# Attention and two expert layers on one core: single conversion steps, a norm by 32x32 transposes, operands split in the first phase

## The chip, the core and the metric

The kernel runs on one core of a Trainium2 chip. The core has five engines with a queue each: TensorE (PE in the rows, its weight loads PEld), VectorE (DVE), ScalarE (ACT), GpSimd (POOL) and SyncE (SP), whose queue issues the DMAs here. Each engine works through its queue in order; an instruction waits for semaphores that others raise. Matrix products write to PSUM, here to tiles of 512 float32 columns. The metric is the device time of one execution in microseconds; the median of three runs of the kernel before is 1184.3 us (1182.97 to 1186.25).

## The reference

```python
def _attn_ref(q, k, v, tau):            # q, k, v: 1 x 6016 x 256
    qn = q / (np.linalg.norm(q, axis=1, keepdims=True) + 1e-06)
    kn = k / (np.linalg.norm(k, axis=1, keepdims=True) + 1e-06)
    s = kn.transpose(0, 2, 1) @ qn / tau
    s = s - s.max(-1, keepdims=True)
    a = np.exp(s)
    a /= a.sum(-1, keepdims=True) + 1e-09
    return (v @ a).astype(np.float32)
# x = _attn_ref(...) as 6016 x 256, then
def _moe_ref(x, w_in, w_out):           # 256 -> 2048 -> 256
    h = np.maximum(x @ w_in, 0.0)
    return (h * h @ w_out).astype(np.float32)
def _moe2_ref(x, w_gate, w_val, w_out, rms_g):   # 256 -> 1536 -> 256
    rms = np.sqrt(np.mean(x * x, axis=-1, keepdims=True) + 1e-06)
    xn = x / rms * rms_g
    g = xn @ w_gate
    silu = g * (1.0 / (1.0 + np.exp(-g)))
    return (silu * (xn @ w_val) @ w_out).astype(np.float32)
```

`w_in`, `w_out`, `w_gate`, `w_val` and the second `w_out` (`w2` in the kernel) arrive as float64 and are converted on the chip.

## The kernel before

**Precision.** A float32 product is made of three products of rounded halves: `mm3` (L95 to L98) multiplies the high half of the weights by the high and by the low half of the data, then the low half of the weights by the high half of the data. A high half is a cast to `fp32r` (ACT), a low half the difference between the value and its cast (DVE): the helper `split`, L91 to L93.

**Start.** `q` and `k` are read in chunks and give the 256 x 256 scores; the softmax gives the matrix `a`. Since `v @ a @ w_in` is linear up to the relu, `a` is multiplied into `w_in` (`emit_m`, tiles `m_h`, `m_l`).

**Weights.** Each piece of a float64 weight goes through five stages (class `Call`): `load` (SP), `a` (POOL and ACT take the two words of each number), `b` in three DVE instructions `b0`, `b1`, `b2`, `h` (the high half, ACT) and `l` (the low half, DVE). Gate and value weights (class `Pieces`) are also combined on POOL into seven blocks (for a scheme of seven instead of eight products of 2 x 2 blocks), of which the first two chunks stay in SBUF and the others are stored to DRAM through the tile `gp` with two buffers. `tick` runs the stages of one weight together.

**First phase.** The 6016 tokens are 12 blocks: ten of 512 and two of 448. A block goes through 16 units (function `unit`, L630 ff.): `up` is one 128-row strip of the hidden layer (6 matmuls), then `read` takes it from PSUM with a relu (ACT, `r`), squares it (`s`, on ACT in odd units, on DVE in even ones) and casts the square (`sh`, ACT); `rest` makes the low half `sl` (DVE, L691); `down` multiplies both into two sums `y` (6 matmuls). `pending` holds `down` back by two units. Blocks 0 and 1 run interleaved, blocks 2 to 11 one after the other. A unit takes further work by `hooks` (ahead of `read`), `mid` (behind it) and, from L700 on, functions returned by the hooks, that run last: the transposes and splits of the next block of `v` (`prep`), `tick` in units 1 and 5, the norm of the block before, and the operands of the pair before.

**Norm and operands.** `norm_steps` copies `y` from PSUM, squares both halves (ACT), adds them (DVE), splits the sum and multiplies it by a matrix of 1/256 (L745, L746, two matmuls of 512 columns), so that each of 128 rows holds the mean; then come a square root (ACT), four reciprocals of a quarter each (L753) and two multiplications (L759). Two blocks make a pair: with four differences on POOL (`pair_steps`, L774) the seven operands of the seven products are complete and are stored to DRAM as one DMA (L780).

**Second phase.** Six pairs, each in 12 groups (function `group`). A group makes seven products of three matmuls (L841) into four banks, combines them on DVE (`u`, `h22`, `h21`, `h12`), applies silu on ACT, and splits the results into `sh` and `sl`; four `down` of three matmuls fall into the group's slots, delayed by some slots. Operands of the next pair are fetched in group 9 as one tile (L811) and split in group 11, each behind its last product, by a cast on ACT and a difference on POOL (`split_op`, L817, L818). The sums of a pair are read from PSUM by DVE transposes (`finish`, L924) in the first two groups of the next pair, two in each.

The order of the work is the order of the Python code: each engine's queue holds its instructions as they are emitted. A tile is given again when all uses of the tile before in the same buffer are done.

## Time and profile before

| | |
|---|---|
| median of three runs | 1184.3 us |
| profiled execution, and its span | 1183.07 us, 1181.3 us |
| busy: TensorE, VectorE, ScalarE, GpSimd | 96%, 75%, 56%, 13% |
| granted TensorE clock, mean | 0.992 of 2.4 GHz |
| DMA | 79.66 MB, mean 67 GB/s |

The span runs from the first to the last instruction of one profiled execution. Lines such as L691 are lines of the kernel before. In the names of tiles, `mm` and `acc` are PSUM banks. By the timeline the start takes about 62 us, the first phase reaches to about 613 us, the second to the end. A row of waits names the instruction that waited, the instruction for which it waited, the total, the number of times and the longest. The clock of a window is the mean of what was granted in it: 1.00 is 2.4 GHz, and 0.50 the lower level, 1.2 GHz.

### The profile page before, as it was taken

To read this page: it belongs to the slowest core of one execution; us is meant where nothing else is said; L and a number is where in the kernel's file an instruction comes from. 1 tells how busy PE (TensorE), PEld (TensorE's weight loads), DVE (VectorE), ACT (ScalarE), POOL (GpSimd) and SP (SyncE) were. 2 spreads that over 40 slices of the span, in tenths; PEclk is the share of its full clock that TensorE was granted. 3 is DMA by queue.
4 is the path that set the end of the run, shared out by engine and by line. 5 is a ranking of instruction groups with operands and counts; after the bars stand their busy time and mean duration, and the time that the engine had idled before them with its cause. 6 is when DMAs were issued, how large, how long until landed. Compare 5 with 4: busy or idle time off the path is not lost.

```text
span 1181.3 us, 14492 instructions
## 1 busy us (share of the span) xinstructions
PE 1136.7 (96%) x5220; PEld 946.0 (80%) x5220; DVE 891.7 (75%) x1319; ACT 661.6 (56%) x1144; POOL 150.6 (13%) x142
## 2 busy tenths in 40 slices
PE   8999979999999999999999999999999999999996
PEld 7978858787887878889987787887887787787895
DVE  7987778766866866665647879779778778878875
ACT  7787778577677576566675344334334334334332
POOL 0121120401201210200211112003003003003000
PEclk9999989999999999999999999999999999999999
DMA  9853332313223120100323303001100200300101
GB/s 291 219 141 90 90 83 79 115 46 117 73 62 98 57 86 16 63 16 1 125 96 154 117 1 90 9 1 38 61 1 19 81 1 4 88 1 1 36 1 32
DMA packets 85289, 79.66 MB, mean 67 GB/s; under 512 B 56032, under 2 KB 70880, under 8 KB 83552
## 3 DMA queue, kind: packets, MB, share of 16 engines
q1 hardware_dynamic: 85216, 78.72, 22.0%
q8 instruction: 41, 0.67, 0.2%
q14 instruction: 32, 0.26, 0.1%
HBM read 54.43 MB, written 24.28 MB: 67 GB/s over the span
## 4 chain that ended last, share of the span: by engine, by line
PE 75%; DVE 10%; issue 5%; ACT 5%; DMA 3%; SPq 2%; POOL 1%; DVEq 0%; ACTq 0%; POOLq 0%
PE mm L841 24%; PE acc L97 10%; PE acc L96 10%; PE acc L98 10%; PE mm L96 6%; PE mm L97 6%; PE mm L98 6%; DVE hp L905 1%; DVE sl L896 1%; DVE hp L882 1%; SPq L325 1%; DVE hp L871 1%; DVE hp L881 1%; DVE pu L869 1%; ACT sh L892 1%
## 5 line engine op out<-in xcount | busy, mean ns | idle before, releaser
L841 PE MATMUL mm<-o,gv 128*128 128x512 f32 (+1 forms) x1512 | 388.7, 388 | 9.6 <-DVE hp L871 5.1
L841 PEld LDWEIGHTS mm<-o,gv 128*128 128x128 f32 x1512 | 283.4, 188 | 70.7 <-DVE hp L871 8.9
L691 DVE TENSOR_TENSOR sl<-o,sh 128x512 fp32r<-128x512 f32 (+1 forms) x192 | 141.3, 736 | 114.9 <-ACT sh L684 102.7
L679 ACT ACTIVATE o<-mm 128x512 f32<-128x512 f32 (+1 forms) x192 | 112.6, 587 | 126.6 <-PE mm L98 125.1
L892 ACT CAST sh<-hp 128x512 fp32r<-128x512 f32 (+1 forms) x144 | 88.2, 612 | 169.7 <-DVE hp L882 102.2
L97 PE MATMUL acc<-sl,wo_h 128*128 128x512 f32 (+1 forms) x384 | 151.4, 394 | 6.2 <-DVE sl L691 6.2
L96 PE MATMUL mm<-o,m_h 128*128 128x512 f32 (+1 forms) x384 | 149.3, 389 | 4.7 <-ACT o L92 4.7
L96 PE MATMUL acc<-sh,wo_h 128*128 128x512 f32 (+1 forms) x384 | 150.1, 391 | 1.5 <-ACT sh L687 1.5
L98 PE MATMUL acc<-sh,wo_l 128*128 128x512 f32 (+1 forms) x384 | 149.2, 388 | 0.2 <-DVE wo_l L160 0.2
L98 PE MATMUL mm<-o,m_l 128*128 128x512 f32 (+1 forms) x384 | 148.8, 388 | 0.3 <-DVE m_l L621 0.3
L97 PE MATMUL mm<-o,m_h 128*128 128x512 f32 (+1 forms) x384 | 149.0, 388 | 0.0
L879 ACT ACTIVATE sg<-mm 128x512 f32<-128x512 f32 (+1 forms) x72 | 42.3, 588 | 136.5 <-PE mm L841 136.5
L896 DVE TENSOR_TENSOR sl<-hp,sh 128x512 fp32r<-128x512 f32 (+1 forms) x144 | 108.5, 754 | 12.0 <-ACT sh L892 7.4
L96 PE MATMUL acc<-sh,w_h 128*128 128x512 f32 (+1 forms) x288 | 112.0, 389 | 4.2 <-DVE ot L924 4.2
L818 POOL TENSOR_TENSOR o<-xs,o 128x512 fp32r<-128x512 f32 (+1 forms) x42 | 60.3, 1461 | 409.5 <-ACT o L817 409.2
L97 PE MATMUL acc<-sl,w_h 128*128 128x512 f32 (+1 forms) x288 | 112.0, 389 | 0.3 <-DVE sl L896 0.2
L98 PE MATMUL acc<-sh,w_l 128*128 128x512 f32 (+1 forms) x288 | 111.0, 385 | 0.0
L97 PEld LDWEIGHTS acc<-sl,wo_h 128*128 128x128 f32 x384 | 72.7, 189 | 21.7 <-DVE sl L691 8.9
L881 DVE TENSOR_TENSOR hp<-mm,pu 128x512 f32<-128x512 f32 (+1 forms) x72 | 48.8, 678 | 54.1 <-PE mm L841 54.1
L96 PEld LDWEIGHTS mm<-o,m_h 128*128 128x128 f32 x384 | 72.6, 189 | 19.6 <-ACT o L92 5.2
L96 PEld LDWEIGHTS acc<-sh,wo_h 128*128 128x128 f32 x384 | 72.7, 189 | 17.4 <-ACT sh L687 3.1
L686 DVE TENSOR_TENSOR o<-o 128x512 f32<-128x512 f32 (+1 forms) x88 | 64.5, 732 | 27.9 <-ACT o L679 26.6
(132 smaller groups left out, 1728.8 us busy)
## 6 DMA issues: line engine op xcount, KB each, us to landing
xd<-xst SPq DMA_DIRECT2D x5, 1792.0 KB, 6.7
raw<-in_moe_w_out_dram SPq DMA_DIRECT2D x14, 512.0 KB, 3.8
gv<-gvd SPq DMA_DIRECT2D x4, 1792.0 KB, 9.8
xs<-xd SPq DMA_DIRECT2D x4, 1792.0 KB, 7.2
gvd<-gp SPq DMA_DIRECT2D x12, 512.0 KB, 3.3
out_dram<-ot SPq DMA_DIRECT2D x40, 128.0 KB, 2.5
qraw<-in_q_dram SPq DMA_DIRECT2D x13, 384.0 KB, 5.3
qraw<-in_k_dram SPq DMA_DIRECT2D x13, 384.0 KB, 6.0
```

Source lines behind the costliest of these rows:

```text
L96: nc.tensor.matmul(o, wh, xh, start=start, stop=False)
L97: nc.tensor.matmul(o, wh, xl, start=False, stop=False)
L98: nc.tensor.matmul(o, wl, xh, start=False, stop=stop)
L679: nc.scalar.activation(out=r, in_=o, func=AF.Relu)
L686: nc.vector.tensor_tensor(out=s, in0=r, in1=r, op=ALU.mult)
L691: nc.vector.tensor_tensor(out=sl, in0=s, in1=f32(sh), op=ALU.subtract)
L818: nc.gpsimd.tensor_tensor(out=ops[i][1], in0=src, in1=f32(ops[i][0]), op=ALU.subtract)
L841: nc.tensor.matmul(bank, c[:, hl, a, fs], x, start=start and j == 0, stop=j == 2, skip_group_check=not start)
L879: nc.scalar.activation(out=sg1, in_=b0, func=AF.Silu)
L881: add(out=h21, in0=b2, in1=u, op=ALU.add)
L892: nc.scalar.copy(out=parts[t][0], in_=x)
L896: dve(out=pl, in0=x, in1=f32(ph), op=ALU.subtract)
```

## The change

- **Mean weight.** `mean_w` becomes a 128 x 128 float32 matrix that sums those partitions whose numbers agree modulo 32, divided by 256; POOL makes it from the identity.
- **Norm.** After the squares and their sum, DVE transposes 32 x 32 blocks and sums each block's rows, which leaves 16 columns (14 in the small blocks); one float32 matmul of 16 columns gives the means. Root and reciprocal are taken of those 16 columns; an ACT copy spreads each over 32 columns, a DVE transpose turns it back.
- **Conversion.** From block 2 on `small_steps` gives one step of the conversion to each unit, as last work (`beside`, behind `rest`), in place of `tick`. `down` is held back by three units.
- **Operands.** The differences of a pair move from POOL to DVE, and each operand is split in the first phase: a cast (ACT) and a difference (DVE) into the tile `ys` with two buffers, then a store of 512 KB for each operand. In blocks 3, 5, 7, 9 and 11 this is the work of units 0 to 7.
- **Second phase.** Operands are loaded as halves: three of the next pair in group 4 (group 10 in the first pair), four behind their last product in group 11. `split_op` is gone.
- **Sums.** ACT copies the last sums of a pair to SBUF, also to `ys`, behind their last matmul; the four transposes read that copy, one in each of groups 1 to 4.

```diff
+            self.made = []
+            return [f for j in range(self.np) for f in (lambda j=j: self.hi_of(j), lambda j=j: self.lo_of(j))]
...
+    def small_steps():
+        for i in range(state["b"], len(calls)):
+            c = calls[i]
+            def start(i=i):
+                upto("h", i)
+                upto("l", i)
+                upto("a", i + 1)
+            def bits(c=c):
+                c.b0()
+                c.b1()
+            def whole(i=i, c=c):
+                c.b2()
+                state["b"] = i + 1
+                if not c.keeps_raw:
+                    upto("load", i + 1 + NRAW)
+            def through(i=i, c=c):
+                state["h"] = state["l"] = i + 1
+                upto("load", i + 1 + NRAW)
+            yield from [start, bits, whole]
+            hl = c.hl_steps()
+            for f in hl[:-1]:
+                yield f
+            yield lambda f=hl[-1], through=through: (f(), through())
...
-        upto("h", state["b"])
+        if not beside:
+            upto("h", state["b"])
+        for h in beside:
+            h()
...
-            for d, x in enumerate((st["rms"], q)):
+                w = vp.tile([P, 2, NB], F32, tag="vraw", name="w")[:, :, :n]
+                st["w"] = [w[:, 0], w[:, 1]]
+            for d, x in enumerate(st["w"]):
                 nc.scalar.activation(out=x, in_=slot(d), func=AF.Square)
-            nc.vector.tensor_tensor(out=st["rms"], in0=st["rms"], in1=q, op=ALU.add)
         def s2():
-            st["rr"] = xp.tile([P, 2, NB], F32R, tag="rr", name="rr")[:, :, :n]
-            split(st["rms"], st["rr"][:, 0], st["rr"][:, 1])
+            w, q = st["w"]
+            nc.vector.tensor_tensor(out=w, in0=w, in1=q, op=ALU.add)
+            nc.vector.transpose(out=q.rearrange("p (g t) -> p g t", t=32), in_=w.rearrange("p (g t) -> p g t", t=32))
         def s3():
-            ms = mm()[:, :n]
-            nc.tensor.matmul(ms, mean_w, st["rr"][:, 0], start=True, stop=False)
-            nc.tensor.matmul(ms, mean_w, st["rr"][:, 1], start=False, stop=True)
-            return lambda: nc.scalar.activation(out=st["rms"], in_=ms, func=AF.Sqrt, bias=eps)
-        def s4(i):
-            def f():
-                w = n // 4
-                ap = st["rms"][:, i * w : (i + 1) * w]
-                nc.vector.reciprocal(out=ap, in_=ap)
-            return f
-        def s5(d):
+            x = norm_small.tile([P, 2, NB // 32], F32, tag="ns", name="ns", bufs=2)
+            if n < NB:
+                nc.gpsimd.memset(x, 0.0)
+            st["sm"] = [x[:, i, :G] for i in range(2)]
+            nc.vector.tensor_reduce(
+                out=st["sm"][0], in_=st["w"][1].rearrange("p (g t) -> p g t", t=32), axis=AX.X, op=ALU.add
+            )
+        def s4():
+            ms = mm()[:, :G]
+            nc.tensor.matmul(ms, mw, st["sm"][0], start=True, stop=True)
+            def root():
+                x, r = st["sm"]
+                nc.scalar.activation(out=x, in_=ms, func=AF.Sqrt, bias=eps)
+                nc.vector.reciprocal(out=r, in_=x)
+            return root
+        def s5():
+            w, q = (x.rearrange("p (g t) -> p g t", t=32) for x in st["w"])
+            nc.scalar.copy(out=q, in_=st["sm"][1].unsqueeze(2).to_broadcast([P, G, 32]))
+            nc.vector.transpose(out=w, in_=q)
+        def s6(d):
             def f():
                 nc.vector.scalar_tensor_tensor(
-                    out=slot(d), in0=slot(d), scalar=g_sb[:, d : d + 1], in1=st["rms"], op0=ALU.mult, op1=ALU.mult
+                    out=slot(d), in0=slot(d), scalar=g_sb[:, d : d + 1], in1=st["w"][0], op0=ALU.mult, op1=ALU.mult
                 )
             return f
-        return [s0], [s1, s2, s3, s4(0), s4(1), s4(2), s4(3), s5(0), s5(1)]
+        return [s0], [s1, s2, s3, s4, s5, s6(0), s6(1)]
...
+                nc.vector.tensor_tensor(out=x[0], in0=x[1], in1=x[2], op=ALU.subtract)
             return f
-        def store():
-            x_dram[p] = dp.tile([P, NC7, NB], F32, tag=f"x{p}", name="xd")
-            nc.sync.dma_start(out=x_dram[p][:, :, :n], in_=xst[p][:, :, :n])
-        return [sub(3, 2, 0), sub(1, 6, 3), sub(2, 6, 2), sub(5, 4, 1), store]
+        def hi(i):
+            def f():
+                st[i] = xp.tile([P, 2, NB], F32R, tag="ys", name="xp", bufs=2)[:, :, :n]
+                nc.scalar.copy(out=st[i][:, 0], in_=xst[p][:, i, :n])
+            return f
+        def lo(i):
+            def f():
+                t = st.pop(i)
+                nc.vector.tensor_tensor(out=t[:, 1], in0=xst[p][:, i, :n], in1=f32(t)[:, 0], op=ALU.subtract)
+                if p not in x_dram:
+                    x_dram[p] = dp.tile([P, NC7, 2, NB], F32, tag=f"x{p}", name="xd")
+                nc.sync.dma_start(out=x_dram[p][:, i, :, :n], in_=f32(t))
+            return f
+        def both(*fs):
+            return lambda: [f() for f in fs] and None
+        return [
+            both(hi(0), sub(3, 2, 0)), both(lo(0), hi(3), sub(1, 6, 3)), both(lo(3), hi(1), sub(2, 6, 2)),
+            both(lo(1), hi(2), sub(5, 4, 1)), both(lo(2), hi(4)), both(lo(4), hi(5)), both(lo(5), hi(6)),
+            both(lo(6)),
...
-    def fetch(p):
+    def fetch(p, i, ops):
         n = blocks[2 * p][1]
-        if p == 0:
-            w = [wp.tile([P, 2, NB], F32, tag="raw", name="xs", bufs=NRAW) for _ in range(3)]
-            w = [x[:, i] for x in w for i in range(2)] + [wp.tile([P, NB], F32, tag="dg", name="xs", bufs=3)]
-            for i, x in enumerate(w):
-                nc.sync.dma_start(out=x[:, :n], in_=x_dram[p][:, i, :n])
-            return [x[:, :n] for x in w]
-        t = xp.tile([P, NC7, NB], F32, tag="xst", name="xs")
-        nc.sync.dma_start(out=t[:, :, :n], in_=x_dram[p][:, :, :n])
-        return [t[:, i, :n] for i in range(NC7)]
-    def split_op(src, ops, i):
-        n = src.shape[-1]
+        if i < 3 and p % 2:
+            if i == 0:
+                ops["x"] = xp.tile([P, NC7, NB], F32R, tag="xst", name="xs")
+            ops[i] = ops["x"][:, 2 * i, :n], ops["x"][:, 2 * i + 1, :n]
+            nc.sync.dma_start(out=f32(ops["x"])[:, 2 * i : 2 * i + 2, :n], in_=x_dram[p][:, i, :, :n])
+            return
         ops[i] = place(2 * i)[:, :n], place(2 * i + 1)[:, :n]
-        nc.scalar.copy(out=ops[i][0], in_=src)
-        nc.gpsimd.tensor_tensor(out=ops[i][1], in0=src, in1=f32(ops[i][0]), op=ALU.subtract)
+        for j in range(2):
+            nc.sync.dma_start(out=f32(ops[i][j]), in_=x_dram[p][:, i, j, :n])
...
+                if f == NF2 - 1 and p < NP - 1:
+                    if d == 0:
+                        o[t] = xp.tile([P, KC, NB], F32, tag="ys", name="ys", bufs=2)
+                    nc.scalar.copy(out=o[t][:, d, :n], in_=o[t, d])
...
+            hooks = merge(hooks, {8: n0}, at_steps(n1, 9))
         else:
             n0, n1 = norm_steps(b - 1, ys[b - 1])
-            hooks = merge({6: n0}, at_steps(n1, 7))
             if b % 2:
-                hooks = merge(hooks, at_steps(pair_steps(b // 2 - 1), 1))
-        if b + 1 < NBLK:
+                hooks = merge({8: n0}, at_steps(n1, 9))
+                beside = merge(beside, at_steps(pair_steps(b // 2 - 1), 0))
+            else:
+                hooks = merge({3: n0}, at_steps(n1, 4))
+        if not last:
             s = prep(b + 1)
-            hooks = merge(hooks, {0: [load(b + 1)]} if b > 2 else {}, {3: s[:1], 4: s[1:2], 8: s[2:3], 9: s[3:]})
+            hooks = merge(hooks, {0: [load(b + 1)]} if b > 2 else {})
+            beside = merge(beside, {6: s[:1], 7: s[1:2], 13: s[2:3], 14: s[3:]})
+            for u in range(UNITS):
+                beside.setdefault(u, []).extend(conv_steps(1))
         else:
-            hooks = merge(hooks, {8: [lambda: xs0.extend(fetch(0))]})
-        mid = {1: [tick], 5: [tick]} if b + 1 < NBLK else {}
+            beside = merge(beside, {13: [lambda: [fetch(0, i, ops0) for i in range(3)]]})
+        for u in range(UNITS):
+            beside.setdefault(u, []).append(lambda: None)
         up, down, ys[b] = mlp1(b, vts[b], lambda f: f % 2 == 1)
-        run(up, down, NF1, 2, merge(hooks), mid)
-    assert state["b"] == len(calls) == state["l"]
+        run(up, down, NF1, 3, hooks, {}, beside)
...
+    for i in range(3, NC7):
+        fetch(0, i, ops0)
...
-                split_op(xs[p + 1][i], new, i)
+            if f == NF2 - 1 and p + 1 < NP and i > 2:
+                fetch(p + 1, i, nxt)
...
-            if f == 9 and p + 1 < NP:
-                xs[p + 1] = fetch(p + 1)
+            if f == (10 if p == 0 else 4) and p + 1 < NP:
+                for i in range(3):
+                    fetch(p + 1, i, nxt)
...
-            if tails and f < 2:
-                tails[1](f)
-        tails = [left.pop(), finish]
-        ops = new
+            if tails and 1 <= f < 5:
+                tails[1][f - 1]()
+        tails = [left.pop(), finish(0) + finish(1)]
```

ACT's queue in block 3, units 1 and 2, before: `o6`, `o7` are the relu's outputs, `o8` the square, `gp` the buffer of weight pieces on their way to DRAM. The last `gp` waits for a store.

```order
L679 ACTIVATE o6_2267<-mm_2259 128x512 [waits PE_49]
L683 ACTIVATE o8_2268<-o6_2267 128x512 [waits DVE_49,Activation_49]
L684 CAST sh_2269<-o8_2268 128x512 [waits Activation_49]
L126 ACTIVATE raw_1870<-raw_1870 128x512 [waits DMAHW6_49,Pool_49]
L194 CAST gp_2285<-dg_1975 128x256 [waits DVE_49]
L194 CAST gp_2289<-raw_1868 128x512 [waits DMAHW0_49,Pool_49]
L194 CAST gp_2293<-raw_1868 128x512 [waits DMAHW5_49,DVE_49,Pool_49]
L679 ACTIVATE o7_2311<-mm_2303 128x512 [waits PE_49]
```

The same place now, units 1 to 3; `xp` is an operand's halves in one of the two buffers.

```order
L737 ACTIVATE o6_2289<-mm_2282 128x512 [waits PE_49]
L741 ACTIVATE o8_2290<-o6_2289 128x512 [waits DVE_49,Activation_49]
L742 CAST sh_2291<-o8_2290 128x512 [waits Activation_49]
L854 CAST xp_2300<-xst_1777 128x512 [waits DVE_49]
L198 CAST gp_2303<-raw_1896 128x512 [waits DMAHW1_49,Pool_49]
L737 ACTIVATE o7_2318<-mm_2311 128x512 [waits PE_49]
L745 ACTIVATE sh_2320<-o7_2318 128x512 [waits Activation_49]
L854 CAST xp_2328<-xst_1777 128x512 [waits DMAHW7_49,DVE_49]
L737 ACTIVATE o6_2348<-mm_2341 128x512 [waits PE_49]
L741 ACTIVATE o8_2349<-o6_2348 128x512 [waits Activation_49]
L742 CAST sh_2350<-o8_2349 128x512 [waits Activation_49]
L854 CAST xp_2358<-xst_1777 128x512 [waits DMAHW0_49,DVE_49]
```

Three casts of weight pieces stood together behind unit 1; now one stands there, and behind each unit one cast of a pair operand, of which those from unit 2 on wait for a DMA.

TensorE's queue in block 3 around the norm's product, before: `m_h`, `m_l` are the weights of `up`, `wo_h` of `down`.

```order
L98 MATMUL mm_2489<-o12_2046,m_l_757 128x512
L745 MATMUL mm_2496<-rr_2466,mean_w_75 128x512 [waits Activation_49]
L746 MATMUL mm_2496<-rr_2466,mean_w_75 128x512 [waits DVE_49]
L96 MATMUL acc0_2319<-sh_2447,wo_h_81 128x512
L97 MATMUL acc0_2319<-sl_2448,wo_h_81 128x512
```

And now:

```order
L106 MATMUL mm_2587<-o12_2189,m_l_769 128x512
L815 MATMUL mm_2594<-ns_2569,mean_w_75 128x16 [waits DVE_49,Activation_49]
L104 MATMUL acc0_2364<-sh_2522,wo_h_93 128x512 [waits Activation_49]
L105 MATMUL acc0_2364<-sl_2523,wo_h_93 128x512
L106 MATMUL acc0_2364<-sh_2522,wo_l_94 128x512
```

Two matmuls of 512 columns, fed by two halves, became one of 16, fed by the reduction.

ACT's queue at a change of pairs in the second phase, before: `pu` and `sg` are the copies and silus of a group, `sh` its casts, `o2` to `o12` the operands of the next pair.

```order
L863 COPY pu_7263<-mm_7260 128x512 [waits PE_49]
L902 ACTIVATE sg_7257<-sg_7257 128x512 [waits DVE_49,Activation_49]
L817 CAST o2_7284<-xs_7198 128x512 [waits PE_49,Pool_49]
L892 CAST sh_7289<-hp_7205 128x512 [waits DVE_49]
L817 CAST o4_7296<-xs_7198 128x512 [waits PE_49,Pool_49]
L817 CAST o6_7308<-xs_7198 128x512 [waits PE_49,Pool_49]
L817 CAST o8_7319<-xs_7198 128x512 [waits PE_49,Pool_49]
L879 ACTIVATE sg_7323<-mm_7260 128x512 [waits PE_49,Activation_49]
L817 CAST o10_7328<-xs_7198 128x512 [waits PE_49,Pool_49]
L817 CAST o12_7340<-xs_7198 128x512 [waits PE_49,Pool_49]
```

And now, at a change of pairs:

```order
L953 COPY pu_7488<-mm_7484 128x512 [waits PE_49]
L992 ACTIVATE sg_7482<-sg_7482 128x512 [waits DVE_49,Activation_49]
L982 CAST sh_7506<-hp_7414 128x512 [waits DVE_49]
L920 COPY ys_7525<-acc0_6827 128x512 [waits PE_49]
L969 ACTIVATE sg_7530<-mm_7484 128x512 [waits PE_49,Activation_49]
L920 COPY ys_7525<-acc1_6841 128x512 [waits PE_49]
L982 CAST sh_7555<-hp_7489 128x512 [waits DVE_49]
L953 COPY pu_7550<-mm_7547 128x512 [waits PE_49]
L992 ACTIVATE sg_7544<-sg_7544 128x512 [waits DVE_49,Activation_49]
L920 COPY ys_7564<-acc0_6867 128x512 [waits PE_49]
```

The casts of operands are gone; two copies of finished sums stand before the silu and behind it, a third in the next group.

## Rows read from the trace of the kernel before

**Rows 1.** Page, part 1: busy time, share of the span, instructions.

```profile
PE 1136.7 (96%) x5220; PEld 946.0 (80%) x5220; DVE 891.7 (75%) x1319; ACT 661.6 (56%) x1144; POOL 150.6 (13%) x142
```

**Rows 2.** Timeline of TensorE, first phase: start us, us, line, operation; 88 matmuls apart.

```profile
459.83 0.39 PE L96 MATMUL mm<-o,m_h 128*128 128x512 f32 x1
...
479.87 0.39 PE L98 MATMUL mm<-o,m_l 128*128 128x512 f32 x1
```

**Rows 3.** What TensorE waited for, 163 to 613 us: total, times, longest.

```profile
PE mm L96 <- ACT o L92: 4.7, 1, 4.7
PE acc L97 <- DVE sl L691: 4.0, 4, 2.8
PE acc L96 <- ACT sh L687: 1.5, 2, 0.7
```

**Rows 4.** Chain of waits, 222 to 231 us: start us, us, what.

```profile
222.40 2.47 DMA gvd<-gp
...
224.96 0.63 ACT gp L194
...
226.66 1.70 DVE o L686
...
228.47 1.55 DVE sl L691
```

**Rows 5.** Windows: us, busy PE, PEld, DVE, ACT, POOL, granted clock, DMA share, GB/s.

```profile
224.00:236.00 12.00, 9.23 (x34) 7.02 (x33) 9.41 (x12) 6.05 (x11) 6.53 (x5) 0.86 0.73 262
236.00:608.00 372.00, 368.77 (x1649) 308.92 (x1648) 246.47 (x351) 251.35 (x439) 43.87 (x36) 1.00 0.19 61
608.00:622.00 14.00, 12.23 (x50) 10.25 (x49) 5.08 (x8) 9.29 (x16) 7.41 (x6) 0.88 0.63 255
```

**Rows 6.** What TensorE waited for, 608 to 1181 us.

```profile
PE mm L841 <- DVE hp L871: 5.1, 8, 1.1
PE acc L96 <- DVE ot L924: 4.2, 5, 0.9
...
PE mm L841 <- ACT o L817: 1.1, 1, 1.1
PE mm L841 <- POOL o L818: 0.6, 1, 0.6
```

**Rows 7.** Timeline of POOL and of DVE at a change of pairs.

```profile
706.93 9.31 POOL L818 TENSOR_TENSOR o<-xs,o 128x512 fp32r<-128x512 f32 x6 [0.75 <-ACT o L817]
...
711.74 1.64 DVE L882 TENSOR_TENSOR hp<-sg,hp 128x512 f32<-128x512 f32 x1
713.30 0.68 DVE L886 TENSOR_TENSOR sg<-mm,pu 128x512 f32<-128x512 f32 x1
```

**Rows 8.** Timeline of TensorE: the same wait at two changes of pairs.

```profile
729.67 0.47 PE L96 MATMUL acc<-sh,w_h 128*128 128x512 f32 x1 [0.82 <-DVE ot L924]
...
822.97 0.47 PE L96 MATMUL acc<-sh,w_h 128*128 128x512 f32 x1 [0.82 <-DVE ot L924]
```

**Rows 9.** Lines by shape: count, busy us, mean ns, idle before and its cause.

```profile
L679 ACT ACTIVATE o<-mm 128x512 f32<-128x512 f32 x160 | 95.2, 595 | 100.3 <-PE mm L98 100.2
...
L683 ACT ACTIVATE o<-o 128x512 f32<-128x512 f32 x88 | 55.7, 633 | 2.6
L684 ACT CAST sh<-o 128x512 fp32r<-128x512 f32 x88 | 54.6, 621 | 2.8
...
L504 PE MATMUL mm<-ones,ws 128*128 128x1 f32 x8 | 0.9, 239 | 0.0
```

**Rows 10.** DMA issues: count, KB each, median us to landing.

```profile
xd<-xst SPq DMA_DIRECT2D x5, 1792.0 KB, 6.7
...
xs<-xd SPq DMA_DIRECT2D x4, 1792.0 KB, 7.2
gvd<-gp SPq DMA_DIRECT2D x12, 512.0 KB, 3.3
...
gvd<-gp SPq DMA_DIRECT2D x4, 256.0 KB, 2.4
```

## What was predicted

> **What bounds the kernel.** I read the share of busy time first: TensorE 96%, VectorE (DVE) 75% [rows 1]. Then the timeline of TensorE in an undisturbed stretch of the first phase: 88 matmuls between the two rows take 20.04 us, so a matmul of 512 columns costs 0.2277 us and TensorE stops nowhere [rows 2]. A unit of the first phase (12 matmuls) is therefore 2.73 us, a pair of blocks in the second phase (12 groups of 33 matmuls) 90.2 us. The end is set by TensorE's queue; a change can only take matmuls away, or remove or add places where TensorE waits. So the rest of the reading is a list of such places.
>
> In blocks 2 to 11 TensorE waits for the differences `sl` (L691) and the casts `sh` (L687) [rows 3]. The chain of waits at the largest of these shows why: a store of a weight piece has to land before ScalarE (ACT) can cast the next piece into the same buffer; behind that stand, on DVE, a multiply of 1.70 us and the `sl` that TensorE needs, 1.55 us [rows 4]. Such a stop costs more than itself: in 224 to 236 us the granted clock is 0.86 of 2.4 GHz, a part of it at 1.2 GHz, 12 x 0.14 = 1.7 us. The same at the entry to the second phase: 0.88 over 14 us, 1.7 us [rows 5].
>
> In the second phase TensorE waits for `hp`, and once each for the operand split on ACT and on GpSimd (POOL) [rows 6]. The timeline at a change of pairs gives the reason: POOL makes six operand differences in a row, and beside them a DVE product of two SBUF tiles takes 1.64 us, where the next instruction, with an operand in PSUM, takes 0.68 us [rows 7]. A wait for `ot`, the transposed output, follows; from that wait at one change of pairs to the same at the next 93.30 us pass [rows 8], 3.1 us more than the 90.2 us of matmuls.
>
> **The change, part by part.** Each gain is a stop in the trace that loses its cause.
>
> A. Conversion in single steps, one in each unit, and a third `down` held back instead of two. The casts and differences of one weight no longer stand together ahead of `sh` and `sl`. By the busy times TensorE stood 12.00 - 9.23 = 2.8 us in the stretch with the longest stop and 372.00 - 368.77 = 3.2 us in all the rest up to 608 us; with the clock's 1.7 us that is 7.7 us [rows 5]. I take 8. The 4.7 us stop at L96 [rows 3], around 163 us, belongs to the last units of blocks 0 and 1, whose order does not change; it stays.
>
> B. The norm. 24 matmuls of 448 or 512 columns go: at 0.2277 us about 5.4 us. Twelve products of 16 or 14 columns come. No row shows that shape; the nearest are products of one column, 0.239 us busy each, pipelined [rows 9]. Between nothing and 0.24 us each, that is 0 to 2.9 us; I take 1.4, so 4 us gained. Transposes, reduction and the ACT copy lie beside matmuls; they matter only for how late the product's input is (F).
>
> C. Entry to the second phase. Operands arrive split, so the waits for L817 and L818 go, 1.1 + 0.6 us [rows 6], with the clock of 1.7 us [rows 5]: 3.4 us, of which I take 3.
>
> D. Changes of pairs. POOL has nothing left to do there, so DVE goes back to 0.68 us; ACT copies the sums out, so the first sums of a pair no longer wait for `ot` [rows 8]; the four transposes are spread over four groups. Five changes at about 3.1 us are 15.5 us; some waits for `hp` follow from DVE's own load, so I take 13. In return four operands come by eight loads issued when their last product has been read. Counted in products of 0.68 us, the first is free 4.1 us into the last group, the last must be there at 14.3 us. These 2 MB in 10.2 us stand against 1.75 MB in 7.2 us [rows 10], that is 8.2 us. They are hidden, with about 2 us to spare: cost 0. If that cover is gone, each change loses up to the 3 us that it gained.
>
> E. Pair 0 of the second phase. The last norm and the last pair's operands run beside its first eight groups. DVE gets eleven instructions of 0.6 us (0.68 x 448/512) that POOL had or nobody, loses four reciprocals, and in groups 4 to 7 two casts follow a store into the same buffer within one group. I take -1 us, between +4 (the old waits there vanish) and -5 (both casts hold ACT for a whole store).
>
> F. The new wait. Pair operands are cast into two buffers in turn, `ys`. In the order of the third block a cast of unit u+2 waits for a DMA: the store of unit u+1's buffer. Work out one turn on ACT from the `relu` of the unit whose difference fills the buffer: relu 0.595, square 0.633, cast 0.621 [rows 9], then on DVE `sl` and the operand's difference at 0.68 each [rows 7], then the store of 512 KB, 3.3 us from issue to landing [rows 10], then the next cast 0.62. That is 7.1 us for what should take two units, 5.46 us. ACT falls 1.65 us behind in each turn; behind that cast on ACT stand the next `relu`, square and `sh`, for which DVE and TensorE wait. Three turns (operands 1, 4 and 6) make 5 us by unit 6. What can TensorE bear? `sl` has a margin of over 5 us, since three `down` are held back. The tighter place is the norm's product after unit 12: its reduction stands on DVE behind the multiply, difference and conversion step of unit 10. Unit 10's relu starts 24.6 us after that of unit 1, and 0.6 + 5 x 0.7 us later the reduction is done, at 28.7; the product's turn is at 30.0. So about 1.5 to 2 us are free, and about 3 us of each odd block reach TensorE. There are five odd blocks, the last without weights to convert: I take 14 us.
>
> Bounds for F: with the landing of a 256 KB store, 2.4 us [rows 10], a turn is 6.2 us, three turns give 2.2 us, and 0 to 3 us are lost in all. At the other end stands a whole 1,792 KB store, 6.7 us: a turn of 10.5, 15 us behind, 13 us a block, 65 us. I take the row of the same size.
>
> Nothing else reaches TensorE: the weight of the mean is built on POOL in the first microseconds and first used after 150 us. Moving the pair differences from POOL to DVE costs 24 x 0.68 = 16 us of an engine with 25% free, beside matmuls.
>
> **Sum.** 8 + 4 + 3 + 13 - 1 - 14 = 13 us. The profiled execution took 1183.07 us, 1.8 us more than its span; 1183.1 - 13 = 1170. The median of the runs, 1184.3, lies 1.2 us higher, so 1171.
>
> **Rivals.**
> 1. The ring does no harm: stores of 4 KB rows land nearer 2.5 us, or ACT's slack swallows the delay. For it: ACT is busy 56% over the span, and TensorE's margin at `sl` is over 5 us. Against it: the profile before already has such a wait for a store in front of its longest stop [rows 4]. Then F is 2 and the sum 25: 1159 us.
> 2. The ring decides and the kernel gets slower. The place is the cast of the third, fifth and seventh operand in odd blocks. The stores share the DMA queue with weight-piece stores, weight loads and `v` loads. Each turn that is later than 7.1 us adds three times its delay to a block. All other terms are 27 us, or 5.4 us a block, so beyond 5.4 + 1.7 = 7.1 us behind, a landing of about 4 us, the change is a loss. At 5 us a turn is 8.8, three turns 10 us, 8.3 a block, 42 in all: 15 us slower, 1199. For it: DMA is up to 0.73 busy where such stores stood together [rows 5]. Against it: 3.3 us is the median of twelve such stores. The Trainium skill ("DMA: Bandwidth & Descriptors", section "Latency and other measured facts") gives the access latency of HBM as 0.2 us on average and 2 us at high load; by that rule these stores would land about 1.8 us later, near this rival's 5 us; the trace of before shows no such store under this load.
> 3. The changes of pairs keep their 3 us, since the eight loads are late (2 us of room) or `hp` stays late from DVE's own load. Then D is 0 and so is the sum: 1184 us, no difference.
>
> **How the numbers follow.** The forecast has a chance of 0.50, with its own range 1163 to 1180 (F from 8 to 20, E from +2 to -4). Rival 1 has 0.25, rival 2 0.13, rival 3 0.12. A measurement of this kernel tells about 0.3%, 3.6 us, from no change: faster is below 1180.7, slower above 1187.9. Faster: 0.48 + 0.25 + 0.03 = 0.76. Same: 0.02 + 0.02 + 0.08 = 0.12. Slower: 0.11 + 0.01 = 0.12. The range that leaves out two in ten runs from rival 1's middle, 1155, to above rival 3, 1187.
>
> **What would show it.** Right: at 222 to 232, 286, 366 and 423 us no wait for L691 or L687; POOL idle in the second phase, DVE's differences at 0.68 us there, a pair in 90 to 91 us; in odd blocks waits of ACT for the store of `xp`, growing to about 5 us of delay by unit 6, and TensorE waiting up to 3 us for the reduction at the norm's product. Wrong: no such wait at the product (rival 1), TensorE waiting for `sl` from unit 5 on (rival 2), waits of L931 for loads of `o` at changes of pairs (rival 3). I would be most wrong if ACT took up the turns, since F is the largest single cost and the only one not seen before.

## The result, and the profile after

The changed kernel takes 1196.5 us (median of four runs, 1195.3 to 1197.9), the kernel before 1183.6 beside it: 1.0108 times as long, 95% interval 1.0084 to 1.0131. It is slower by 12.9 us where 1171 us, 13 us faster, was forecast. The profiled execution has a span of 1194.6 us.

TensorE is still what the end hangs on; GpSimd (POOL) has lost two thirds of its work. Page, part 1, of the changed kernel (busy time, share of the span, instructions), beside [rows 1]:

```profile
PE 1149.8 (96%) x5220; PEld 950.6 (80%) x5220; DVE 868.9 (73%) x1372; ACT 669.6 (56%) x1164; POOL 55.2 (5%) x91
```

TensorE is busy for 13.1 us more with as many instructions. The timeline of TensorE shows a part of the reason in a stretch where it stops nowhere (start us, us, line, operation; 96 matmuls, that is 8 units, between the two rows):

```profile
289.00 0.39 PE L104 MATMUL mm<-o,m_h 128*128 128x512 f32 x1
...
311.13 0.39 PE L104 MATMUL mm<-o,m_h 128*128 128x512 f32 x1
```

22.13 us for 96 is 0.2305 us each, where [rows 2] gave 0.2277. The slower step is there in every stretch of 50 us, also in blocks 0 and 1, where the order of the work did not change. This was not in the forecast at all.

What TensorE waited for, 163 to 613 us (total, times, longest), beside [rows 3]:

```profile
PE mm L815 <- ACT gp L198: 5.6, 1, 5.6
PE mm L104 <- ACT o L100: 4.7, 1, 4.7
PE mm L815 <- DVE ns L809: 4.1, 1, 4.1
PE mm L815 <- ACT sh L745: 3.5, 2, 1.8
PE acc L105 <- DVE sl L749: 0.2, 1, 0.2
```

The waits for `sl` and `sh` at a `down` are gone, as step A said; the one for `o` stayed. New are four stops at the norm's product, L815, one in each of blocks 3, 5, 7 and 9; block 11 has the fifth, below.

The chain of waits into the first of them (start us, us, what):

```profile
226.98 0.62 ACT xp L854
...
228.15 3.77 DMA xd<-xp
...
232.00 0.62 ACT xp L854
...
234.34 0.62 ACT xp L854
...
235.82 2.87 DMA xd<-xp
...
238.77 0.62 ACT xp L854
...
243.17 1.08 ACT xst L787 x2
...
253.98 0.63 ACT gp L198
...
254.69 0.58 PE mm L815 x2
```

A cast into one buffer follows the cast before into the same buffer after 7.4 and 6.8 us (226.98 to 234.34, 232.00 to 238.77); two units should take 5.5. ScalarE falls behind by its waits for these stores (total, times, longest, 222 to 256 us), and the copies of `y` (L787) and the product behind them come late:

```profile
ACT xp L854 <- DMA xd<-xp: 7.4, 4, 2.7
```

The windows (us; busy PE, PEld, DVE, ACT, POOL; granted clock, DMA share, GB/s) right after stops, and at the entry to the second phase, whose first product starts at 630.91 us, beside [rows 5]:

```profile
254.00:266.00 12.00, 11.31 (x42) 9.23 (x43) 8.00 (x14) 7.64 (x14) 0.00 (x0) 0.80 0.48 133
440.00:456.00 16.00, 14.25 (x57) 11.25 (x56) 10.18 (x17) 9.56 (x17) 0.00 (x0) 0.89 0.00 1
624.00:640.00 16.00, 15.69 (x71) 12.74 (x69) 5.77 (x9) 7.64 (x13) 0.00 (x0) 1.00 0.55 181
```

After each of the five stops TensorE runs for a while at 1.2 GHz. The stop of 1.75 us at 440 us costs another 16 x 0.11 = 1.8 us that way, about as much as itself. From 163 to 613 us the mean clock is 0.97, before it was 0.99. The entry runs at full clock, as step C said.

What TensorE waited for from 613 us on, beside [rows 6]:

```profile
PE mm L815 <- ACT sh L745: 3.0, 1, 3.0
PE mm L931 <- DVE hp L961: 2.9, 3, 1.0
PE acc L104 <- ACT sh L982: 2.5, 2, 1.5
PE acc L105 <- DVE sl L986: 0.6, 3, 0.2
PE mm L931 <- DMA o<-xd: 0.5, 2, 0.3
```

No wait for `ot` is left. The waits for `hp` L961 and `sh` L982 all lie before 700 us, in pair 0, where the last operands go through the same two buffers. Behind that a window as long as the old pair period [rows 8] shows TensorE without a stop:

```profile
712.00:805.00 93.00, 93.00 (x403) 75.51 (x402) 73.16 (x115) 37.60 (x65) 0.00 (x0) 1.00 0.18 52
```

DMA issues (count, KB each, us to landing), beside [rows 10]: the store that was taken as 3.3 us lands in 2.6 in the median; the late loads of operands, at 4.8, are hidden but for the 0.5 us of waits above.

```profile
xd<-xp SPq DMA_DIRECT2D x35, 512.0 KB, 2.6
o<-xd SPq DMA_DIRECT2D x58, 256.0 KB, 4.8
```

So two things want a cause: the stops with what hangs on them, and a slower step in every stretch.

### The profile page after: what moved, and what is told of

Its sections match the earlier page's. It is cut to its first block, busy times and chain, and to the rows that moved or that the text cites. A ratio compares the mean times of both kernels' runs of the same rounds, so it can differ in the third digit from the quotient of the medians.

```text
span 1194.6 us, 14612 instructions
## 1 busy us (share of the span) xinstructions
PE 1149.8 (96%) x5220; PEld 950.6 (80%) x5220; DVE 868.9 (73%) x1372; ACT 669.6 (56%) x1164; POOL 55.2 (5%) x91
## 4 chain that ended last, share of the span: by engine, by line
PE 72%; ACT 10%; DVE 8%; DMA 5%; issue 3%; SPq 1%; POOL 1%; DVEq 0%; ACTq 0%; POOLq 0%
PE mm L931 26%; PE acc L104 10%; PE acc L106 10%; PE acc L105 10%; PE mm L104 5%; PE mm L105 5%; PE mm L106 5%; DMA xd<-xp 4%; ACT o L737 2%; ACT o L741 2%; ACT sh L742 1%; DVE xp L861 1%; ACT xp L854 1%; SPq L380 1%; DVE sl L749 1%
## 5 line engine op out<-in xcount | busy, mean ns | idle before, releaser
L931 PE MATMUL mm<-o,gv 128*128 128x512 f32 (+1 forms) x1188 | 313.8, 391 | 3.4 <-DVE hp L961 2.9
L931 PEld LDWEIGHTS mm<-o,gv 128*128 128x128 f32 x1188 | 222.5, 188 | 54.3 <-DVE hp L961 5.2
L749 DVE TENSOR_TENSOR sl<-o,sh 128x512 fp32r<-128x512 f32 (+1 forms) x192 | 132.9, 692 | 144.5 <-ACT sh L742 132.8
L982 ACT CAST sh<-hp 128x512 fp32r<-128x512 f32 (+1 forms) x144 | 88.1, 612 | 152.1 <-DVE hp L972 98.1
L104 PE MATMUL mm<-o,m_h 128*128 128x512 f32 (+1 forms) x384 | 151.1, 393 | 4.7 <-ACT o L100 4.7
L104 PE MATMUL acc<-sh,wo_h 128*128 128x512 f32 (+1 forms) x384 | 153.5, 400 | 0.0
L106 PE MATMUL acc<-sh,wo_l 128*128 128x512 f32 (+1 forms) x384 | 151.8, 395 | 0.2
L105 PE MATMUL mm<-o,m_h 128*128 128x512 f32 (+1 forms) x384 | 150.4, 392 | 0.1
L986 DVE TENSOR_TENSOR sl<-hp,sh 128x512 fp32r<-128x512 f32 (+1 forms) x144 | 96.4, 669 | 10.3 <-ACT sh L982 6.3
L104 PEld LDWEIGHTS mm<-o,m_h 128*128 128x128 f32 x384 | 73.8, 192 | 19.6 <-ACT o L100 5.2
L106 PEld LDWEIGHTS acc<-sh,wo_l 128*128 128x128 f32 x384 | 73.4, 191 | 16.8 <-DVE wo_l L171 0.9
L105 PEld LDWEIGHTS mm<-o,m_h 128*128 128x128 f32 x384 | 73.5, 191 | 15.6 <-DVE o L101 0.9
L106 PEld LDWEIGHTS mm<-o,m_l 128*128 128x128 f32 x384 | 73.4, 191 | 15.6 <-DVE m_l L676 1.0
```

Of the source, the lines that this page charges most:

```text
L104: nc.tensor.matmul(o, wh, xh, start=start, stop=False)
L105: nc.tensor.matmul(o, wh, xl, start=False, stop=False)
L106: nc.tensor.matmul(o, wl, xh, start=False, stop=stop)
L749: nc.vector.tensor_tensor(out=sl, in0=s, in1=f32(sh), op=ALU.subtract)
L931: nc.tensor.matmul(bank, c[:, hl, a, fs], x, start=start and j == 0, stop=j == 2, skip_group_check=not start)
L982: nc.scalar.copy(out=parts[t][0], in_=x)
```

## The experiments

Each group ran on one chip beside runs of the kernel before (1183.2 to 1184.0 us).

### The two buffers

`ring`: halves of pair operands in tiles of their own, each stored at once. The memory is the same.

```diff
-st[i] = xp.tile([P, 2, NB], F32R, tag="ys", name="xp", bufs=2)[:, :, :n]
-nc.scalar.copy(out=st[i][:, 0], in_=xst[p][:, i, :n])
+st[i] = xp.tile([P, NB], F32R, tag="yh", name="xph", bufs=2)[:, :n]
+nc.scalar.copy(out=st[i], in_=xst[p][:, i, :n])
+nc.sync.dma_start(out=x_dram[p][:, i, 0, :n], in_=f32(st[i]))
...                      # the low half likewise: tag "yl", its own store;
                         # the copies of the sums use yh and yl too
```

> The changed kernel with the pair operands' high and low halves in tiles of their own, two of each kind in the same memory, each half stored as soon as it is made; a cast then waits only for a store issued two units earlier. Theory F (the ring of two buffers made ScalarE late, and the norm's product with it): the five stops at that product, 16.2 us in all, go, and the granted clock from 163 to 613 us returns from 0.97 to 0.99, another 9 us: about 1171 us. Rival B (the odd blocks carry too much work for ScalarE and VectorE, whatever the buffers): at least 10 us of those stops stay, in place of DMA waits of ScalarE; 1190 us or more.

Measured: 1168.2 us, 28.3 below the changed kernel (0.9865 of before, 0.9851 to 0.9880). TensorE's waits, 163 to 613 us:

```profile
PE mm L104 <- ACT o L100: 4.8, 1, 4.8
PE mm L815 <- ACT gp L198: 1.5, 1, 1.5
PE mm L815 <- DVE ns L809: 1.0, 1, 1.0
```

In block 3 ScalarE waits for stores:

```profile
ACT xph L854 <- DMA xd<-xph: 1.3, 1, 1.3
```

The five stops have shrunk from 16.2 to 2.5 us, and these waits from 7.4 us to 1.3. Rival B falls: the work in the odd blocks is the same, and it fits. Of the 28.3 us, 23.8 lie in the first phase (569.8 us from the first `up` to the first product of the second phase, now 546.0). 13.7 of these are the stops. Some 10 are left, and the lower clock behind the five stops accounts for about 9: 12 x 0.20 = 2.4 us in the first window above, and 1.7 or 1.8 us behind each of the other four. Pair 0 of the second phase is 5.7 us shorter, 95.8 instead of 101.4 us between the first products of pairs 0 and 1 (the first phase of `ring` began 0.9 us later). In the changed kernel and in `ring`:

```profile
630.91 0.86 PE L931 MATMUL mm<-o,gv 128*128 128x512 f32 x3
...
732.35 0.87 PE L931 MATMUL mm<-xs,gv 128*128 128x512 f32 x3
```

```profile
607.99 0.86 PE L933 MATMUL mm<-o,gv 128*128 128x512 f32 x3
...
703.74 0.86 PE L933 MATMUL mm<-xs,gv 128*128 128x512 f32 x3
```

### The slower step

Between the kernels the widths of four small tiles had changed, `eps`, `g_sb`, `tau_sb` and `rden`, from 64 to 128 bytes of each partition, and with them the place of all tiles behind them; the parts of the diff above do not show these lines. Three kernels undo or redo that alone, the third in part:

```diff
# lay_narrow: the changed kernel          # lay_wide: the kernel before, the reverse
-eps = wp.tile([P, 32], F32, name="eps")[:, 0:1]
+eps = wp.tile([P, 16], F32, name="eps")[:, 0:1]
...                                       # g_sb, tau_sb, rden likewise
# lay_rden: the changed kernel, rden alone
-rden = wp.tile([P, 32], F32, name="rden")[:, 0:KC]
+rden = wp.tile([P, 16], F32, name="rden")[:, 0:KC]
```

> The changed kernel with its four small tiles (eps, g_sb, tau_sb, rden) 64 bytes wide again instead of 128, so that every large tile stands at the offset it had before. Theory L (the place of the tiles in SBUF sets the step from one matmul to the next): the dense step of 512 columns falls from 0.2306 to 0.2278 us everywhere, about 4,700 steps x 0.0028 = 13 us, so about 1183 us; the stops at the norm's product stay. Rival N (the slower step comes from something else in the change, or from this execution): 0.2306 and about 1196 us.

> The kernel before with nothing changed but the four small tiles, 128 bytes wide instead of 64; no instruction moves. Theory L: the dense step rises from 0.2278 to 0.2306 us, 1183.6 + 13 = about 1197 us. Rival N: 0.2278 and no difference.

> The changed kernel with only the last of the four small tiles (rden) 64 bytes wide. The weights wo and w2 stay at 0 modulo 128 bytes, as in the changed kernel, while the moving data (o, sh, sl) and m go from 0 to 64 modulo 128. If the relative place of weights and data decides (in the kernel before it is 64 against 0), the dense step falls to about 0.228 us and the time to about 1184; if the weights' own place decides, the step stays at 0.2306 and the time at 1196. Rival N: also 0.2306 and 1196.

Measured: `lay_narrow` 1189.2 us, 7.3 below the changed kernel; `lay_wide` 1193.6, 10.0 above the kernel before where 13 were expected (1.0084, 1.0069 to 1.0099); `lay_rden` 1190.2. Rival N falls: without one instruction moved, the kernel before takes the slower step. TensorE's timeline in `lay_wide`, 96 matmuls apart, 22.13 us:

```profile
295.13 0.39 PE L96 MATMUL mm<-o,m_h 128*128 128x512 f32 x1
...
317.26 0.39 PE L96 MATMUL mm<-o,m_h 128*128 128x512 f32 x1
```

Why `lay_narrow` gains less than 10: with a shorter step TensorE reaches the late products earlier; its first four stops there add up to 14.1 us instead of 13.2. The granted clock also falls further: 0.57 instead of 0.79 in 348 to 356 us, 0.79 instead of 1.00 in 684 to 692 us, together at most 3.4 us.

`lay_rden` seemed to say that weights and data must not stand at the same place modulo 128 bytes. Three kernels on top of `ring` move groups of tiles apart:

```diff
# both64: eps, g_sb, tau_sb 64 bytes wide, rden 128
# wts64: the same, and behind the weights wo, w2
+wp.tile([P, 16], F32, tag="pad", name="pad")
# scr64: that pad, eps, g_sb, tau_sb 128 bytes wide, rden 64
```

> The kernel with the split ring, with three small tiles (eps, g_sb, tau_sb) 64 bytes wide and rden 128: now the weights wo, w2 and the moving data o, sh, sl stand all at 64 modulo 128 bytes, where the split ring has both at 0 and the kernel before has 64 and 0. If it is the place of weights and data relative to each other, the dense step stays at 0.2306 us and the time at 1168; if the weights' own place decides, 0.228 and about 1160.

> The kernel with the split ring, where only the weights wo and w2 are moved to 64 modulo 128 bytes (an unused tile of 64 bytes behind them puts every later tile back to 0 modulo 128). Theory W (the weights against the data that TensorE reads): the dense step falls from 0.2306 to about 0.228 us, about 1158 to 1160 us. Theory S (the working tiles raw, dg, sg, pu that ScalarE, VectorE and the DMAs use, against the data): 0.2306 and 1168.

> The reverse: weights wo, w2 and the data o, sh, sl at 0 modulo 128 bytes, the working tiles raw, dg, sg, pu and one weight tile of the second phase (gv0) at 64. Theory S: 0.228 and about 1160 us. Theory W: 0.2306 in the first phase and 1168 us, less what the one gv tile gives in the second phase (at most 2 us).

Measured: 1169.0, 1168.6 and 1166.4 us. `both64` fits "the relative place decides", but neither Theory W nor Theory S holds: `wts64` has the weights alone at 64, and its step is the slowest so far (22.30 us for 96):

```profile
282.57 0.39 PE L104 MATMUL mm<-o,m_h 128*128 128x512 f32 x1
...
304.87 0.39 PE L104 MATMUL mm<-o,m_h 128*128 128x512 f32 x1
```

What orders the mean step of all kernels is the distance from the weights to the data in bytes over a longer period. It was 64, 128 and 192 so far; the next kernels, on both repairs (`ring_narrow`, below), set it to 0 and beyond:

```diff
# dist0: rden is allocated ahead of the weights
 tau_sb = wp.tile([P, 16], F32, name="tau_sb")[:, 0:1]
+rden = wp.tile([P, 16], F32, name="rden")[:, 0:KC]
# dist256, dist448: an unused tile of 192, 384 bytes behind the weights
```

> The kernel with both repairs, with rden (64 bytes) allocated ahead of the weights instead of behind them. The distance from the weights wo to the data o, m, sh shrinks by 64 bytes, from 64 modulo 1024 (dense step 0.228 us) to 0; 128 gave 0.2306 and 192 gave 0.2322 in the runs so far. Theory D (the step depends on that distance, and grows with it): below 0.228, at most 0.227 us, and 1153 to 1156 us. Rival M (weights and data at the same place modulo 128 bytes are slow, as they were in three kernels): here both stand at 0 modulo 128 again, so 0.2306 us and 1167.

> The kernel with both repairs with 192 unused bytes between weights and data: distance 256 modulo 1024. Theory D with a linear growth: 0.233 to 0.234 us and about 1175; if the effect repeats every 256 bytes, this is the same as distance 0.

> The same with 384 unused bytes: distance 448 modulo 1024. If the effect repeats every 512 bytes, this is 64 short of a repeat; Theory D with growth up to the repeat: above 0.234 us; if it repeats every 256 bytes, 448 is like 192: 0.2322 us and about 1168; if it repeats every 128 bytes, like 64: 0.228 and 1158.

Measured: `dist0` 1153.9 us (1151.9 to 1156.6), `dist256` 1155.9 and `dist448` 1169.9 (one run each). The timeline of `dist0`, 96 matmuls, 21.76 us:

```profile
282.49 0.39 PE L105 MATMUL mm<-o,m_h 128*128 128x512 f32 x1
...
304.25 0.39 PE L105 MATMUL mm<-o,m_h 128*128 128x512 f32 x1
```

Theory D holds, rival M falls, and the distances tried fit a period of 256 bytes: 256 is like 0, 448 like 192. The places are those of the built programs, for the weights `wo_h` and the first `sh`:

| kernels | `wo_h`, `sh` at byte | distance modulo 256 | 96 matmuls |
|---|---|---|---|
| `dist0` | 2944, 181120 | 0 | 21.76 us |
| `dist256` | 2880, 181312 | 0 | 21.76 |
| before, `lay_narrow`, `ring_narrow` | 2880, 181120 | 64 | 21.86 |
| `lay_rden` | 3072, 181312 | 64 | 21.87 |
| after, `lay_wide`, `ring`, `scr64` | 3072, 181376 | 128 | 22.13 |
| `both64` | 2880, 181184 | 128 | 22.13 |
| `wts64` | 2880, 181248 | 192 | 22.30 |
| `dist448` | 2880, 181504 | 192 | 22.30 |

At 0, 64 and 128 two different places of the pair give the same step, so there the distance decides and not the place of either.

The traces also tell the two kinds of matmul apart. These are mean steps between successive 512-column matmuls, from their starts in 170 to 600 us, without those over 0.26 us:

| kernel, distance | `up` to `up` | `down` to `down` | from one to the other |
|---|---|---|---|
| `dist0`, 0 | 0.2267 us | 0.2270 us | 0.2268 us |
| before, 64 | 0.2269 | 0.2297 | 0.2262 |
| `lay_wide`, 128 | 0.2276 | 0.2328 | 0.2324 |
| `wts64`, 192 | 0.2316 | 0.2337 | 0.2296 |

In all kernels `m`, `o`, `sh` and `sl` kept their distances among themselves, with `m_h` and the operands `o` at 0 modulo 256. From 0 to 128 it is the steps of `down`, whose weights and data move apart, that slow, and those from one kind to the other; `up` hardly slows. At 192 `up` slows too, though its own operands kept their distance. Both kernels at 192 have `m`, `o` and `sh` at multiples of 256 bytes and no other kernel has, so there the place itself is not told apart from the distance. Why the place matters at all stays open.

### Both repairs, and the parts of the change

`ring_narrow` is `ring` with the four tiles 64 bytes wide. From it parts are undone (the edits in short):

```diff
# tick_back: conversions in one piece, two downs held back
-    beside.setdefault(u, []).extend(conv_steps(1))
-run(up, down, NF1, 3, hooks, {}, beside)
+run(up, down, NF1, 2, hooks, {1: [tick], 5: [tick]}, beside)   # not in the last block
# lag2: only the third down
-run(up, down, NF1, 3, hooks, {}, beside)
+run(up, down, NF1, 2, hooks, {}, beside)
# no_evac: no copies of the sums, transposes from PSUM
-if tails and 1 <= f < 5:
-    tails[1][f - 1]()
+if tails and f < 2:
+    tails[1][2 * f]()
+    tails[1][2 * f + 1]()
```

> Both repairs in the changed kernel: halves of the pair operands in tiles of their own, and the four small tiles 64 bytes wide. If the two costs are independent, the 7.3 us that the narrow tiles gave to the changed kernel come off the 1168.2 us of the kernel with the split ring: 1161 us; with the 10.0 us that they are worth in the kernel before, 1158. Rival: the narrow tiles give nothing once the stops are gone, 1168.

> The kernel with both repairs, but weights converted as before: all stages of one weight together in units 1 and 5, and two downs held back instead of three. Step A of the prediction priced this at 8 us: 8 us above the kernel with both repairs, with waits of TensorE for the low half sl and the cast sh around 226, 286, 366 and 423 us and a store of a weight piece ahead of them on ScalarE. Rival: with the pair operands and the norm elsewhere, those stops do not come back, 0 to 2 us; a third case is more than 12 us, if the conversions in one piece now meet the operand casts and make the norm's product late.

> The kernel with both repairs with single conversion steps, but two downs held back as before. If the third down carries step A (11.7 us measured with both halves undone): about 1168 us, with TensorE waiting for sl in many units; if the single steps carry it: at most 1160 us.

> The kernel with both repairs, but without the ScalarE copies of the sums: the transposes read them from PSUM, two in each of the first two groups of the next pair, as before the change. If these copies carry the gain at the changes of pairs (step D, 13 us), the time rises by about 2 to 3 us at each of five changes, 10 to 15 us, with waits of TensorE for ot; if the idle GpSimd (and VectorE at 0.68 us beside it) carries it, it rises by at most 4 us (five waits of up to 0.9 us).

Measured: `ring_narrow` 1158.0 us (0.9786 of before, 0.9769 to 0.9802), so the narrow tiles keep their 10 us once the stops are gone. `tick_back` 1169.7, 11.7 above it; `lag2` 1160.5, 2.5 above; so four fifths of these 11.7 us are the single steps. TensorE's waits in `tick_back`, 163 to 618 us:

```profile
PE mm L814 <- DVE ns L808: 5.7, 4, 3.7
PE mm L104 <- ACT o L100: 4.8, 1, 4.8
PE acc L105 <- DVE sl L748: 2.9, 4, 1.6
PE acc L104 <- ACT sh L744: 1.0, 2, 0.7
```

The old waits for `sl` and `sh` come back, at 227 to 230, 371 and 428 us; the larger part are waits at the product, partly the third case that was written down. `no_evac`: 1164.2, 6.2 above. Its wait for the transposes is the old one [rows 6]:

```profile
PE acc L104 <- DVE ot L1021: 4.2, 5, 0.9
```

That is between both theories' figures. Of the 6.2 us, 4.8 lie in the second phase of the profiled execution, so the copies carry a third to a half of step D; the share of the idle GpSimd was not tested by itself.

## Why the prediction was wrong

It failed in step F, by its size, and in the sentence "Nothing else reaches TensorE".

- **F, the ring.** The mechanism was right and so was its turn: 7.1 us was forecast, 7.4 and 6.8 stand in the chain, with landings of 3.8 and 2.9 us where 3.3 was taken. ScalarE's waits for stores came to 7.4 us in block 3 where a delay of 5 was forecast. "About 3 us of each odd block" was forecast, and the five stops last 16.2 us, 3.2 each in the mean, though from 1.7 to 5.6. (The prediction's own 28.7 and 30.0 leave 1.3 us free at the product, not 1.5 to 2, which would have made it 18 us instead of 14.) What was mis-sized is the price of a stop. "I take 14 us" counts the stops alone; steps A and C had added the lower clock behind a stop, F did not. With the clock, 9 to 10 us, the ring costs 23.8 us in the first phase, 1.7 times the term, and with pair 0 28.3 in all (`ring`).
- **The step.** The widening of four small tiles is not in the prediction, so it stood at nothing. It is no work, and costs 10.0 us (`lay_wide`), by a mean step that is 1.2% longer. The trace of before held no sign of it, but the whole diff did show that the tiles move.
- **A, conversion.** Forecast 8; undone it costs 11.7, but not by the same stops. The waits for `sl` and `sh`, which A named, come back with 3.9 us; 5.7 us are waits at the norm's product, which A did not name and of which `ring_narrow` has 3.0. So the cause is right, and the size is not shown.
- **B, the norm.** The product is two instructions, and at full clock the next matmul starts 0.22 us after it (`ring`, 341.03 to 341.25 us): 12 of them are 2.6 us against 1.4 taken, inside the bounds.
- **C, the entry.** Right: full clock, 0.5 us of waits for loads.
- **D and E, the second phase.** 12 us together were forecast; from its first product to the end of the span it took 566.7 us before and 552.1 in `ring_narrow`, 14.6 less. Pair 0, where E forecast 1 us more, took 97.3 us before and 96.2 in `ring_narrow`; in the changed kernel, with the ring, it took 101.4, 4.1 more than before and close to the -5 of "both casts hold ACT for a whole store".

All but F and the step were forecast to give 8 + 4 + 3 + 13 - 1 = 27 us; `ring_narrow` is 26.0 below the kernel before. That this comes so near is in part luck: the second phase gave more than its 12 us, and the first, 552.6 us before and 542.2 in `ring_narrow`, gave 10.4 where A, B and C had 15, with 3.0 us of stops still there. From `ring_narrow` to the changed kernel it is 38.5 us, of which the ring is 28.3 or 31.3 and the wide tiles 10.2 or 7.3, by which of the two comes first. The ring alone turns the sign: at the old places of the tiles (`lay_narrow`) the change is still 5.6 us slower than the kernel before.

Of the rivals, 2 came nearest by its sign, but not by its reason: its point was a landing of 4 us or more, and the stores landed in 2.6 in the median. The latency that the Trainium skill ("DMA: Bandwidth & Descriptors", section "Latency and other measured facts") gives for high load did not show in that median. Rival 1 is refuted by the stops, rival 3 by the window of 93 us without one.

The best version is `dist0`: 1153.9 us, 0.9755 of before (0.9733 to 0.9777).

## What to carry to other kernels

Where TensorE is dense, price a stop at its own length and at the time that may follow at the lower clock, in every term alike. A buffer that one engine fills, a second completes and a DMA empties should be split by who fills it, so that each part leaves as soon as it is made. When a change alters the size of any tile, even a small one, compare the step of an undisturbed stretch of matmuls before looking for waits.

## What was not expected of the hardware

- The step of dense 512-column matmuls depends on where weights and data stand in SBUF relative to each other: 21.76, 21.86, 22.13 and 22.30 us for 96 at distances of 0, 64, 128 and 192 bytes modulo 256 between `wo_h` and `sh`, from 0.2267 to 0.2323 us each; up to 128 nearly all of it lies in `down` and in the steps between `down` and `up`. The Trainium skill ("SBUF — State Buffer", section "Who interferes with whom") gives TensorE two independent read ports, for weights and for data, and says that it never waits on anyone. That is said of other engines; taken as a rule for placement as well, it would make the place free, and these runs show that it is not.
- A stop of 1.75 us at 440 us was followed by matmuls at 1.2 GHz, which cost as much again; in `ring`, a stop of 1.5 us was followed by a window at full clock. The length of the stop alone does not tell which: in `lag2` one of 1.7 us at 250 us cost clock, in `dist256` one of 2.5 us at 248 us did not. The windows of `ring`, `lag2` and `dist256`:

```profile
252.00:260.00 8.00, 8.00 (x37) 6.53 (x36) 5.63 (x10) 5.53 (x11) 0.00 (x0) 1.00 0.69 191
252.00:260.00 8.00, 7.88 (x28) 6.35 (x29) 4.80 (x10) 5.20 (x11) 0.00 (x0) 0.79 0.76 198
251.00:259.00 8.00, 8.00 (x36) 6.59 (x36) 5.59 (x11) 5.89 (x11) 0.00 (x0) 1.00 0.81 199
```
